# The first stage of an attention + two-MLP kernel: all its instructions in an order written by a list maker

## The chip, the cores and the metric

The kernel runs on one core of a Trainium2 chip. The metric is device time in microseconds (us) of one execution. Five engines run beside each other, each in its own order: PE (matmul), DVE (vector), ACT (activations), POOL (GpSimd) and SP, which issues most of the transfers (DMAs). PE's weight loads are listed as PEld.

## The reference, cut to what matters

```python
a = softmax(phi, axis=2)                       # (4, 8, 576, 32), over the 576 positions
k_m, v_m = a^T k, a^T v                        # (4, 8, 32, 64): pooled keys and values
attn = softmax(q k_m^T / 8, axis=-1) v_m       # (4, 8, 576, 64) -> x: (2304, 512)
h = x @ w_in;  x = (h * cos(h)) @ w_out        # 512 -> 2048 -> 512; w_in and w_out come as float64
p = domain_probs / sum(domain_probs)           # (2304, 4)
out = sum_e p[:, e] * (relu(x @ w1[e]) @ w2[e])  # 4 experts, 512 -> 1024 -> 512
```

## The kernel before, in words

The work has two stages. **Stage one** holds attention and the cosine MLP. Each of the 4 batches has 8 heads in two groups g of 4 (a *part* is one batch and group, eight in all); the positions of a batch fall into two halves th of 288. For each part `pool_exp` takes the exponential of phi (ACT) and transposes it on PE (tiles `pe`, `pt`, copied to `es`), `pool_kv` pools k and v (`kvp`), scales and turns the result (`kvs`, `pkt`) and copies it to `kT` and `vT` (DVE); `scores` multiplies q by kT (`sc`) and runs the softmax in blocks of 32: DVE transpose, max, POOL subtract, ACT Exp, DVE sum, POOL multiply, DVE transpose, and a split into a high and a low fp32r half, `attnT`. `project` folds v_m into a slice of w_in: v_m times w_in, 256 hidden columns at a time (`vw_ps`, split to `vw`). The MLP has 8 such slices, slots s. A *unit* is one slot, batch and half, 64 in all: `hidden1` makes hp = attnT x vw with 12 matmuls (three products of high and low halves each, `mm3`), then h cos h by a chain ACT, ACT, DVE, ACT (Sin), DVE, and a split into `gt` (ACT high, POOL low); `output1` multiplies by w_out (`wo`), 24 matmuls into `op`, and adds to `acc` in SBUF (DVE). The cosine takes the turns h/2pi, rounds them with a large constant and subtracts.

The float64 weights are brought as pairs of 32-bit words and made float32 by `narrow`: one ACT pass and three DVE passes per piece (L116 to L128); `load_out` also splits wo (`split_w`).

**Stage two** combines x into seven operands (`build_x`: `put` writes `x`, ACT high and DVE low half) and multiplies them with seven combinations of w1 (`load2`, `hidden2`, a scheme with seven products in place of eight), then relu and w2 (`output2`), scaled by p_all on DVE. p_all comes by `load_probs`, a transfer asked for by POOL and four small DVE operations.

What sets the order: the whole program is written in the order of the calls at L375 to L433, and a scheduler with a model of the engines then places every instruction of every engine, within the buffers of the pools. The transfers of the first part of stage one stand on SP's queue, the later weight pieces on ACT's.

The chain of one unit, and the calls that the change touches:

```python
marks.append(nc.scalar.activation(out=y, in_=hv, func=ACTF.Copy, scale=INV_2PI, bias=0.25))   # L320
nc.scalar.activation(out=kk, in_=y, func=ACTF.Copy, bias=ROUND)                               # L321
nc.vector.scalar_tensor_tensor(out=y, in0=kk, scalar=ROUND, in1=y, op0=ALU.subtract, op1=ALU.subtract)  # L322
nc.scalar.activation(out=y, in_=y, func=ACTF.Sin, scale=-TWO_PI)                              # L323
nc.vector.tensor_tensor(out=y, in0=hv, in1=y, op=ALU.mult)                                    # L324
```

Of the kernel before, what the change touches and what calls it, by code (L numbers as in the profile page):

```python
# [11 lines left out]
U32 = mybir.dt.uint32  # L12
I64 = mybir.dt.int64
# [6 lines left out]
TWO_PI = 6.283185  # L20
ROUND = 12582912.0
# [3 lines left out]
def tile_kernel(  # L25
# [81 lines left out]
    def narrow(w, src, after=None, part=None):  # L107
        n, m = w.shape[1:]
        c = 1024 // (2 * m)
        for i in range(0, n, c) if part is None else (part * c,):  # L110
            raw = cw.tile([128, c, 2 * m], U32, tag="raw64", name="raw64")
            with tc.issue_after(after.ins) if after else nullcontext():
                (nc.scalar if after else nc.sync).dma_start(out=raw, in_=src[:, i:i + c])
            lo, hi = (raw.rearrange("p a (b t) -> p a b t", t=2)[:, :, :, t] for t in range(2))
            hif = raw.bitcast(F32).rearrange("p a (b t) -> p a b t", t=2)[:, :, :, 1]
# [13 lines left out]

# [41 lines left out]

    kTs, ees = {}, {}

    def pool_exp(b, g):
        ph = phs[b, g]
        nmx = at.tile([128, 1], F32, tag="nmx", name="nmx", bufs=2)
        nc.vector.tensor_reduce(out=nmx, in_=ph, axis=AX.X, op=ALU.max)
        nc.vector.tensor_scalar_mul(nmx, nmx, -1.0)
        ex = ph
        rs = at.tile([128, 1], F32, tag="rs", name="rs", bufs=2)  # L180
        nc.scalar.activation(out=ex, in_=ph, func=ACTF.Exp, bias=nmx, accum_out=rs)
        nc.vector.tensor_scalar_add(rs, rs, 1e-9)
        nc.vector.reciprocal(out=rs, in_=rs)
        es = at.tile([128, NC + 1, 128], F32, tag="es", name="es", bufs=2)
# [195 lines left out]
    for g in range(2):  # L380
        pool_exp(0, g)
# [289 lines left out]
```

## Time and profile before

| | |
|---|---|
| device time, median of 3 runs | 1185.77 us (1185.19 to 1185.85) |
| device time of the profiled execution | 1186.1 us |
| its span, first to last instruction | 1184.3 us |
| PE busy | 1149.7 us (97%) |
| DVE, ACT, POOL busy | 816.6, 474.0, 520.8 us |
| mean granted TensorE clock | 0.98 |

PE's busy share over the whole span hides that the stages differ: the first 125 us and the rest have to be read apart. A busy microsecond of PE at half the clock does half the work, so the granted clock (1.00 is 2.4 GHz, 0.50 is 1.2 GHz) is read beside it. Lines are those of the kernel before.

### The profile page before, as it was taken

Reading aid. Unit: us, or ns where it says so; the run is one execution under the profiler, and the core shown is the slowest. Engines: PE = TensorE matmul, PEld = TensorE weight load, DVE = VectorE, ACT = ScalarE, POOL = GpSimd, SP = SyncE. Lnnn points to the kernel's source line nnn. Section 1 sums busy time; section 2 is a strip of 40 time slices with the busy share of each in tenths; the row PEclk is TensorE's granted clock in tenths of the full one; section 3 lists DMA queues with packets and bytes.
Section 4 is the critical chain, followed back from the end, with each engine's and each line's share of the span. In section 5 each row is a group of like instructions: output and inputs, shape, how many; then the busy total and the mean of one; then the engine's idle time right before and its main releaser. Section 6 shows DMA issues by size and latency. Waiting matters only on the chain.

```text
span 1184.3 us, 19402 instructions
## 1 busy us (share of the span) xinstructions
PE 1149.7 (97%) x7786; PEld 1029.5 (87%) x7786; DVE 816.6 (69%) x1364; ACT 474.0 (40%) x789; POOL 520.8 (44%) x597
## 2 busy tenths in 40 slices
PE   6798999999999989999999999999999999999998
PEld 4467999999999978989898989898989898989897
DVE  4797778877887796666656665696566666666665
ACT  2866556656666632222222222252222223222320
POOL 1455223323328715445444544465445444544420
PEclk8689999999999999999999999999999999999999
DMA  9830111211121101111111111112111111111102
GB/s 316 296 128 2 37 37 37 72 57 35 53 72 55 54 15 40 36 55 54 36 37 54 54 37 36 54 64 106 37 54 54 37 36 54 55 36 36 54 1 80
DMA packets 38842, 72.85 MB, mean 62 GB/s; under 512 B 2624, under 2 KB 20064, under 8 KB 38752
## 3 DMA queue, kind: packets, MB, share of 16 engines
q1 hardware_dynamic: 34208, 58.99, 15.3%
q10 hardware_dynamic: 4480, 12.58, 3.2%
q8 instruction: 61, 1.00, 0.4%
q0 software_dynamic: 64, 0.04, 0.1%
q14 instruction: 29, 0.24, 0.1%
HBM read 66.88 MB, written 4.72 MB: 60 GB/s over the span
## 4 chain that ended last, share of the span: by engine, by line
PE 83%; DVE 5%; DMA 4%; POOL 3%; ACT 3%; issue 2%; SPq 0%; POOLq 0%; ACTq 0%; DVEq 0%
PE op L132 46%; PE hp L132 35%; DMA raw<-in_w_out_dram 2%; PE vw_ps L288 1%; POOL gt L89 1%; DMA q<-in_qt_dram 1%; POOL wa L505 1%; DVE x L462 1%; DMA kvt<-in_kvt_dram 1%; DVE raw L118 1%; DVE y L324 0%; ACT L323 0%; DVE raw L117 0%; DMA raw<-in_w_in_dram 0%; POOL wo L96 0%
## 5 line engine op out<-in xcount | busy, mean ns | idle before, releaser
L132 PE MATMUL op<-wb,ht 128*128 128x512 f32 x1728 | 439.4, 396 | 0.0
L132 PEld LDWEIGHTS hp<-x,wa 128*128 128x128 f32 x2688 | 380.2, 189 | 25.4 <-DVE x L462 4.1
L132 PE MATMUL hp<-x,wa 128*128 128x256 f32 (+1 forms) x2688 | 393.6, 295 | 4.1 <-DVE x L462 3.4
L132 PEld LDWEIGHTS op<-wb,ht 128*128 128x128 f32 x1728 | 312.7, 188 | 58.4
L594 DVE SCALAR_TENSOR_TENSOR acc<-op,p_all,acc 128x512 f32<-128x512 f32 x270 | 201.7, 748 | 136.2 <-PE op L132 136.1
L132 PE MATMUL op<-gt,wo 128*128 128x288 f32 x1536 | 224.1, 299 | 2.2 <-POOL gt L89 1.2
L132 PEld LDWEIGHTS op<-gt,wo 128*128 128x128 f32 x1536 | 210.4, 189 | 12.2 <-issue 3.9
L96 POOL TENSOR_TENSOR wb<-raw,wb 128x256 fp32r<-128x256 f32 x124 | 90.0, 757 | 223.5 <-ACT wb L94 223.5
L565 ACT ACTIVATE ht<-c 128x256 fp32r<-128x256 f32 (+3 forms) x128 | 71.9, 562 | 283.4 <-DVE c L535 283.4
L89 POOL TENSOR_TENSOR gt<-y,gt 128x576 fp32r<-128x576 f32 x64 | 98.2, 1534 | 174.3 <-ACT gt L88 144.1
L566 DVE SCALAR_TENSOR_TENSOR ht<-c,ht 128x256 fp32r<-128x256 f32 (+3 forms) x128 | 94.0, 735 | 63.8 <-ACT ht L565 63.8
L505 POOL TENSOR_TENSOR wa<-raw,wa 128x256 fp32r<-128x256 f32 x96 | 69.3, 749 | 152.2 <-ACT wa L495 152.2
L132 PE MATMUL hp<-attnT,vw 128*128 128x288 f32 x768 | 117.1, 300 | 5.1 <-DVE y L324 5.1
L535 DVE TENSOR_TENSOR c<-hp,u 128x256 f32<-128x256 f32 (+1 forms) x192 | 87.3, 457 | 42.1 <-PE hp L132 37.9
L132 PEld LDWEIGHTS hp<-attnT,vw 128*128 128x128 f32 x768 | 107.2, 190 | 10.2 <-DVE y L324 6.6
L505 POOL TENSOR_TENSOR wa<-tt,wa 128x256 fp32r<-128x256 f32 x128 | 111.0, 896 | 1.2 <-ACT wa L499 1.2
L346 DVE TENSOR_TENSOR acc<-op,acc 128x576 f32<-128x576 f32 x112 | 83.7, 751 | 24.0 <-PE op L132 22.6
L542 ACT COPY p<-hp 128x256 f32<-128x256 f32 x64 | 25.6, 400 | 108.3 <-PE hp L132 108.3
L322 DVE SCALAR_TENSOR_TENSOR y<-kk,y 128x576 f32<-128x576 f32 x64 | 56.9, 890 | 12.9 <-ACT kk L321 12.3
L495 ACT ACTIVATE wa<-raw 128x512 fp32r<-128x512 f32 x32 | 20.2, 632 | 90.0 <-PE hp L132 88.1
L320 ACT ACTIVATE y<-hp 128x576 f32<-128x576 f32 x64 | 41.4, 647 | 36.1 <-PE hp L132 31.7
L323 ACT ACTIVATE y<-y 128x576 f32<-128x576 f32 x64 | 43.7, 682 | 29.2 <-DVE y L322 29.1
(89 smaller groups left out, 915.5 us busy)
## 6 DMA issues: line engine op xcount, KB each, us to landing
raw<-in_w_dram SPq DMA_DIRECT2D x60, 512.0 KB, 3.5
kv<-in_kv_dram SPq DMA_DIRECT2D x16, 512.0 KB, 8.5
raw<-in_w_in_dram ACTq DMA_DIRECT2D x10, 512.0 KB, 3.3
raw<-in_w_out_dram ACTq DMA_DIRECT2D x10, 512.0 KB, 3.2
q<-in_qt_dram SPq DMA_DIRECT2D x8, 576.0 KB, 7.5
out_dram<-acc SPq DMA_DIRECT2D x18, 256.0 KB, 2.0
raw<-in_w_in_dram SPq DMA_DIRECT2D x6, 512.0 KB, 7.2
raw<-in_w_out_dram SPq DMA_DIRECT2D x6, 512.0 KB, 4.9
```

Source lines behind the costliest of these rows:

```text
L89: (eng or nc.vector).tensor_tensor(out=lo, in0=src, in1=f32(hi), op=ALU.subtract)
L96: (nc.vector if early and c % 512 else nc.gpsimd).tensor_tensor(out=t[:, 1, c:c + 256], in0=src[:, c:c + 256], in1=f32(t[:, 0, c:c + 256]) ...
L132: nc.tensor.matmul(out=ps, lhsT=lt(a), rhs=rt(b), start=first and i == 0, stop=last and i == 2, skip_group_check=more,)
L320: marks.append(nc.scalar.activation(out=y, in_=hv, func=ACTF.Copy, scale=INV_2PI, bias=0.25))
L322: nc.vector.scalar_tensor_tensor(out=y, in0=kk, scalar=ROUND, in1=y, op0=ALU.subtract, op1=ALU.subtract)
L323: nc.scalar.activation(out=y, in_=y, func=ACTF.Sin, scale=-TWO_PI)
L346: nc.vector.tensor_tensor(out=dst, in0=op[:, :, :TH], in1=dst, op=ALU.add)
L505: pool.tensor_tensor(out=wa[:, 1, o], in0=src, in1=f32(wa[:, 0, o]), op=ALU.subtract)
L535: nc.vector.tensor_tensor(out=out, in0=ps[:, :n], in1=sb, op=ALU.add)
L565: nc.scalar.activation(out=ht[:, 0, fc, lo:], in_=c[:, fc, lo:], func=ACTF.Relu)
L566: nc.vector.scalar_tensor_tensor(out=ht[:, 1, fc, lo:], in0=c[:, fc, lo:], scalar=0.0, in1=f32(ht[:, 0, fc, lo:]), op0=ALU.max, op1=ALU.su ...
L594: nc.vector.scalar_tensor_tensor(out=dst, in0=op, scalar=pe, in1=dst, op0=ALU.mult, op1=ALU.add)
```

## The change

The scheduler's order of stage one is replaced. Stage one is now written as tasks, Python generators: `queue` (all transfers, on SP), `part` for each of the eight parts, `narrow_in`, `narrow_out`, `project` and `half` for each unit. Each yields its next step as an `Op` (engine, a duration in ns, what it depends on) or a `Ring` (a place in a buffer pool). `Order.run` keeps a clock per engine in the build, always takes the step that can start first, lets one of a lower rank go ahead if it could start within half of the other's duration (not on PE), and emits it; the instructions of each engine stand in that order (`manual_schedule`). `QUEUE` is the order of the first transfers (p phi, k kv, q q, i w_in, o w_out), written out by hand, `RANKS` that of the first tasks. Stage two is left to the scheduler as before.

Beside the order, single steps change. `narrow` loses one of its three DVE passes: the ACT pass is a Prelu that scales positive and negative high words differently, so that one shift-and-or gives the word with its sign. The cosine's turns are rounded by writing `kk` as int32 from hp (ACT), and DVE subtracts it from hp + 0.25; the factor 1/2pi sits in `vw`, 2pi in the last product, so one ACT pass goes. k and v are copied together into `kvT`, the scale of the scores moves into the Exp; the maximum of phi is negated where it is made. For the first slot the op blocks are copied to acc by DVE or ACT, whichever is free. wo's low half is made by POOL in all slots. `load_probs` moves behind the last unit.

```diff
+QUEUE = """p01 i00 p00 k001 i01 k000 q00 k010 o00 k011 q01 q11 p10 k100 k111 o01 q10 i10 k101 p11
+p20 k110 p21 k200 i11 k201 k301 q21 k211 p30 o11 q20 o10 q31 k300 q30 k210 k310 k311 p31""".split()
+RANKS = "u10 A10 A00 A11 A01 u01 wo0 u00 u20 wi1 P1 A20 P0 wi0 A31 P23 u11 A21 A30 u21 wo1".split()
+RINGS = dict(phi=3, kv=4, q=4, raw=2, wi=2, wf=1, wo=2, es=2, st=2, stT=1, kvs=1, vw=2, y=2, kk=1, gt=3, h=2, o=2, c=2, p2=2)
+WAIT = {"PE": 0.0, "ACT": 0.5, "DVE": 0.5, "POOL": 0.5, "SP": 0.5}
...
+            t, _, eng, task = min(heads, key=lambda h: h[:2])
+            edge = t + WAIT[eng] * task[2].ns
+            for t2, rank, eng2, task2 in heads:
+                if eng2 == eng and rank < task[0] and t2 < edge:
+                    t, task = t2, task2
+                    break
...
-            nc.scalar.activation(out=hif, in_=hif, func=ACTF.Copy, scale=2.0 ** -112)
-            nc.vector.tensor_single_scalar(lo, lo, 29, op=ALU.logical_shift_right)
-            nc.vector.scalar_tensor_tensor(
-                out=lo, in0=hi, scalar=3, in1=lo, op0=ALU.logical_shift_left, op1=ALU.bitwise_or
-            )
-            nc.vector.scalar_tensor_tensor(
-                out=w[:, i:i + c].bitcast(U32),
-                in0=hi,
-                scalar=0x80000000,
-                in1=lo,
-                op0=ALU.bitwise_and,
-                op1=ALU.bitwise_or,
-            )
+        o1 = yield Op(
+            "ACT", 690, lambda: nc.scalar.activation(
+                out=hif, in_=hif, func=ACTF.Prelu, scale=2.0 ** -112, alpha=2.0 ** 32), t)
+        o2 = yield dve(430, lambda: nc.vector.tensor_single_scalar(lo, lo, 29, op=ALU.logical_shift_right), t,
+                       port=True)
+        o3 = yield dve(685, lambda: nc.vector.scalar_tensor_tensor(
+            out=w[:, i * c:i * c + c].bitcast(U32), in0=hi, scalar=3, in1=lo,
+            op0=ALU.logical_shift_left, op1=ALU.bitwise_or), o1, o2, *deps, port=True)
...
+        o = yield dve(420, lambda: nc.vector.tensor_copy(
+            out=kvT[b][p0:p0 + 64], in_=pkt[p0:p0 + 64].rearrange("p u (i m) -> p u i m", i=HG)), o)
...
+        o = yield Op("ACT", 650, lambda: marks.append(
+            nc.scalar.activation(out=kk, in_=hv, func=ACTF.Copy, bias=0.25)), o, t0)
...
+        o = yield dve(755, lambda: nc.vector.scalar_tensor_tensor(
+            out=y, in0=hv, scalar=0.25, in1=kk, op0=ALU.add, op1=ALU.subtract), o, t0)
...
+        o = yield act(685, y, y, ACTF.Sin, o, table="sin", scale=SIN_2PI)
+        o = yield dve(755, lambda: nc.vector.scalar_tensor_tensor(
+            out=y, in0=hv, scalar=TWO_PI, in1=y, op0=ALU.mult, op1=ALU.mult), o)
...
+    with tc.manual_schedule():
+        warm_up(25)
+        todo.at["PE"] = 8500.0
+        todo.add(-1, queue())
...
+        todo.run(lambda: all(("part", b, g) in done for b in range(B) for g in range(2)))
...
+        todo.run()
+        load_probs()
```

Where instructions now stand, at three places.

PE, the stretch that ends with the first op blocks (kvp pools k and v, sc are scores, hp and op the two products of a unit, pe and pt the transposes of phi, pkt that of the pooled k and v). Before, from the pooling of batch 2 on:

```order
L202 MATMUL kvp<-kv,es 32x128 x16
L202 MATMUL kvp<-kvt,es 32x128 x4
L218 MATMUL pkt<-ident,kvs 128x128 x2
L202 MATMUL kvp<-kv,es 32x128 x16
L202 MATMUL kvp<-kvt,es 32x128 x4
L240 MATMUL sc<-q,kT 32x288 x8
L218 MATMUL pkt<-ident,kvs 128x128 x2
L187 MATMUL pe<-ident,phi 128x128 x4
L132 MATMUL op<-gt,wo 128x288 x6
```

And now, up to the pooling of batch 2, group 0:

```order
L233 MATMUL hp<-attnT,vw 128x288 x12
L441 MATMUL pkt<-ident,kvs 128x128 x2
L471 MATMUL sc<-q,kvT 32x288 x4
L534 MATMUL vw_ps<-wi,kvT 32x256 x8
L233 MATMUL op<-gt,wo 128x288 x12
L471 MATMUL sc<-q,kvT 32x288 x4
L534 MATMUL vw_ps<-wi,kvT 32x256 x16
L233 MATMUL op<-gt,wo 128x288 x30
L393 MATMUL pe<-ident,phi 128x128 x4
L233 MATMUL op<-gt,wo 128x288 x6
L400 MATMUL pt<-ident,phi 64x128
L419 MATMUL kvp<-kv,es 32x128 x16
```

48 op matmuls, which stood behind both poolings of batch 2, now stand ahead of the first of them.

SP, the end of the first transfers (raw64 are pieces of w_in and w_out; a tile's number only tells it from others of its name). Before, with kv_730 and kv_734 for batch 3, group 0, and kv_867 and kv_871 for its group 1:

```order
L113 DMA raw64_518<-in_w_out_dram 128x1024
L162 DMA kv_730<-in_kv_dram 128x1024
L162 DMA kv_734<-in_kv_dram 128x1024
L164 DMA kvt_732<-in_kvt_dram 64x256
L164 DMA kvt_736<-in_kvt_dram 64x256
L113 DMA raw64_524<-in_w_out_dram 128x1024
L162 DMA kv_867<-in_kv_dram 128x1024
L162 DMA kv_871<-in_kv_dram 128x1024
L164 DMA kvt_869<-in_kvt_dram 64x256
L164 DMA kvt_873<-in_kvt_dram 64x256
L113 DMA raw64_1549<-in_w_in_dram 128x1024
```

And now, with kv_736 for batch 3, group 0, kv_753 for batch 2, group 1, and kv_886 and kv_901 for batch 3, group 1:

```order
L258 DMA q_609<-in_qt_dram 128x1152
L258 DMA kv_736<-in_kv_dram 128x1024
L258 DMA kvt_737<-in_kvt_dram 64x256
L258 DMA q_746<-in_qt_dram 128x1152
L258 DMA kv_753<-in_kv_dram 128x1024
L258 DMA kvt_754<-in_kvt_dram 64x256
L258 DMA kv_886<-in_kv_dram 128x1024
L258 DMA kvt_887<-in_kvt_dram 64x256
L258 DMA kv_901<-in_kv_dram 128x1024
L258 DMA kvt_902<-in_kvt_dram 64x256
L258 DMA phi_920<-in_phi_dram 128x576
L258 DMA raw64_924<-in_w_in_dram 128x1024
```

The transfers are the same ones. What moved is that all weights of the first two slots now stand ahead of these rows, that q and phi come as late as the kv they belong to, and that pieces of batches 2 and 3 alternate.

DVE, the change of stage (acc is the sum of stage one, x the operands of stage two, p_sum and p_all the probabilities). Before:

```order
L346 TENSOR_TENSOR acc<-op,acc 128x2x288 x5
L462 TENSOR_TENSOR x_0_4703<-acc,x_0_4703 128x512
L462 TENSOR_TENSOR x_5_4710<-sB,x_5_4710 128x512
L462 TENSOR_TENSOR x_4_4713<-sA,x_4_4713 128x512
L475 TENSOR_TENSOR sB<-acc,sB 128x512
L462 TENSOR_TENSOR x_3_4721<-acc,x_3_4721 128x512
L454 TENSOR_TENSOR sA<-acc 128x512
L462 TENSOR_TENSOR x_1_4724<-acc,x_1_4724 128x512
```

And now:

```order
L642 TENSOR_TENSOR acc<-op,acc 128x2x288 x4
L204 TENSOR_REDUCE p_sum<-p_all 128x18
L717 TENSOR_TENSOR x_0_4604<-acc,x_0_4604 128x512
L205 TENSOR_SCALAR p_sum<-p_sum 128x18
L717 TENSOR_TENSOR x_5_4611<-sB,x_5_4611 128x512
L206 RECIPROCAL p_sum<-p_sum 128x18
L717 TENSOR_TENSOR x_4_4614<-sA,x_4_4614 128x512
L717 TENSOR_TENSOR x_3_4622<-acc,x_3_4622 128x512
L730 TENSOR_TENSOR sB<-acc,sB 128x512
L207 TENSOR_TENSOR p_all<-p_all,p_sum 128x72
L717 TENSOR_TENSOR x_1_4625<-acc,x_1_4625 128x512
```

The four operations on the probabilities, which stood among the first dozen of DVE's list, now stand between the x tiles; the reduction of p_all is ahead of all of them.

## Rows read from the trace of the kernel before

**Rows 1.** Windows: us busy of PE, PEld, DVE, ACT, POOL; granted clock, DMA share, GB/s.

```profile
0.00:50.00 50.00, 36.55 (x367) 23.91 (x367) 29.46 (x87) 25.44 (x45) 13.42 (x22) 0.78 0.98 323
50.00:75.00 25.00, 19.93 (x172) 12.13 (x166) 23.54 (x48) 14.57 (x25) 17.45 (x16) 0.61 0.67 230
75.00:125.00 50.00, 44.90 (x418) 38.40 (x417) 37.05 (x65) 37.49 (x53) 26.05 (x19) 0.97 0.01 1
125.00:400.00 275.00, 272.71 (x2315) 259.88 (x2315) 220.80 (x308) 171.25 (x256) 114.43 (x94) 1.00 0.16 53
```

**Rows 2.** Windows: the tile hp alone (two rows), then the tile op.

```profile
0.00:60.00 60.00, 4.56 (x24) 3.48 (x24) 1.49 (x2) 1.27 (x2) 0.74 0.92 307
60.00:125.00 65.00, 19.07 (x108) 16.47 (x108) 5.96 (x8) 5.80 (x9) 0.90 0.17 54
...
60.00:125.00 65.00, 26.63 (x165) 24.22 (x166) 10.88 (x21) 0.90 0.17 54
```

**Rows 3.** Timeline of PE: start, us, instructions merged.

```profile
64.79 1.81 PE L132 MATMUL op<-gt,wo 128*128 128x288 f32 x6 [0.57 <-DVE rs L182]
...
76.16 0.60 PE L187 MATMUL pe<-ident,phi 128*128 128x128 f32 x4
76.69 1.17 PE L240 MATMUL sc<-q,kT 64*32 64x288 f32 x16
...
78.03 1.08 PE L202 MATMUL kvp<-kv,es 128*32 128x128 f32 x32
79.04 0.42 PE L202 MATMUL kvp<-kvt,es 64*32 64x128 f32 x8
...
97.08 1.10 PE L288 MATMUL vw_ps<-wi,vT 64*32 64x256 f32 x32
...
114.32 8.15 PE L132 MATMUL op<-gt,wo 128*128 128x288 f32 x60
```

**Rows 4.** Groups by line, whole span: count, busy us and mean ns, idle before.

```profile
L89 POOL TENSOR_TENSOR gt<-y,gt 128x576 fp32r<-128x576 f32 x64 | 98.2, 1534 | 174.3 <-ACT gt L88 144.1 <-issue 27.6 <-PE op L132 2.5
...
L322 DVE SCALAR_TENSOR_TENSOR y<-kk,y 128x576 f32<-128x576 f32 x64 | 56.9, 890 | 12.9 <-ACT kk L321 12.3 <-POOL wa L505 0.3
L324 DVE TENSOR_TENSOR y<-hp,y 128x576 f32<-128x576 f32 x64 | 47.9, 749 | 8.7 <-ACT y L323 7.8
L321 ACT ACTIVATE kk<-y 128x576 f32<-128x576 f32 x64 | 43.7, 683 | 1.5
L323 ACT ACTIVATE y<-y 128x576 f32<-128x576 f32 x64 | 43.7, 682 | 29.2 <-DVE y L322 29.1
...
L320 ACT ACTIVATE y<-hp 128x576 f32<-128x576 f32 x64 | 41.4, 647 | 36.1 <-PE hp L132 31.7 <-POOL gt L89 4.3
```

**Rows 5.** The same view: the DVE pass of the narrowing that goes.

```profile
L118 DVE SCALAR_TENSOR_TENSOR raw<-raw 128x512 uint32<-128x512 uint32 x32 | 23.6, 736 | 0.6 <-ACT raw L116 0.4
```

**Rows 6.** Groups by line from 0 to 130 us: the table loads.

```profile
L323 ACT ACT_TABLE_LOAD x6 | 7.7, 1283 | 0.1
L254 ACT ACT_TABLE_LOAD x4 | 5.1, 1283 | 0.1
L181 ACT ACT_TABLE_LOAD x2 | 2.6, 1283 | 3.7 <-DMA phi<-in_phi_dram 3.7
```

**Rows 7.** Timeline at the change of stage: POOL, DVE, PE.

```profile
410.52 1.44 POOL L89 TENSOR_TENSOR gt<-y,gt 128x576 fp32r<-128x576 f32 x1 [1.14 <-ACT gt L88]
...
416.00 0.76 DVE L346 TENSOR_TENSOR acc<-op,acc 128x576 f32<-128x576 f32 x1 [0.84 <-PE op L132]
...
421.02 3.84 PE L132 MATMUL hp<-x,wa 128*128 128x256 f32 x18 [1.92 <-DVE x L462]
```

**Rows 8.** Timeline of DVE: the longest of the four on the probabilities.

```profile
10.22 0.27 DVE L82 RECIPROCAL p_sum<-p_sum 128x18 f32<-128x18 f32 x1
```

**Rows 9.** DMA issues: count, KB each, us from issue to landing.

```profile
out_dram<-acc SPq DMA_DIRECT2D x18, 256.0 KB, 2.0
...
p_all<-in_probs_dram POOLq DMA_DIRECT2D x1, 36.0 KB, 8.4
```

More of the change, by code (lines that the diff above doesn't have):

```diff
@@ L19, with __init__, free, take @@
 INV_2PI = 1.0 / (2.0 * math.pi)
-TWO_PI = 6.283185
-ROUND = 12582912.0
+TWO_PI = 2.0 * math.pi
+SIN_2PI = 6.283185
+LOG = []
+class Op:
+    def __init__(self, eng, ns, fn, *deps, table=None, port=False):
+        self.engs = eng.split("|")
+        self.ns, self.fn, self.table, self.port = ns, fn, table, port
+        self.ready = max([0.0, *(d.end if isinstance(d, Op) else d for d in deps)])
+class Ring:
+    def __init__(self, n):
+        self.n, self.ends = n, []
+    def free(self):
+        k = len(self.ends) - self.n
+        return k < 0 or self.ends[k] is not None
+    def take(self):
+        k = len(self.ends) - self.n
+        self.ends.append(None)
+        return len(self.ends) - 1, 0.0 if k < 0 else self.ends[k]
+    def give(self, k, end):
+        self.ends[k] = end.end if isinstance(end, Op) else end
+    def idle(self):
+        return all(e is not None for e in self.ends)
@@ L226, in scores, with have, sp, act @@
-    def scores(b, g, split_th):
-        aT, p0 = attnT[b], 64 * g
-        kT = kTs[b]
+    todo = Order()
+    done = {}
+    marks = []
+    def have(*keys):
+        return Until(lambda: all(k in done for k in keys))
+    def sp(out, in_, nbytes, *deps):
+        return Op("SP", nbytes * DMA_NS, lambda: nc.sync.dma_start(out=out, in_=in_), *deps)
+    def act(ns, out, in_, func=ACTF.Copy, *deps, table=None, **kw):
+        return Op("ACT", ns, lambda: nc.scalar.activation(out=out, in_=in_, func=func, **kw), *deps, table=table)
@@ new lines, in dve, with pool, load @@
+    def dve(ns, fn, *deps, port=False):
+        return Op("DVE", ns, fn, *deps, port=port)
+    def pool(ns, fn, *deps):
+        return Op("POOL", ns, fn, *deps, port=True)
+    R = {name: Ring(n) for name, n in RINGS.items()}
+    tiles = {}
+    def load(ring, key, shape, parts, pool_=None, dtype=F32, tag=None, bufs=None):
+        k, t0 = yield R[ring]
+        pool_ = pool_ or at
+        name = tag or ring
+        t = pool_.tile(shape, dtype, tag=name, name=name, **({"bufs": bufs} if bufs else {}))
+        tiles[key] = t, ring, k
+        op = None
+        for out, in_, nbytes in parts(t):
+            op = yield sp(out, in_, nbytes, t0)
+        done[key] = op.end
@@ new lines, in tile_kernel, with narrow_part @@
+    wi, wo = {}, {}
+    def narrow_part(kind, s, i, w, *deps):
+        yield have((kind, s, i))
+        raw, ring, k = tiles[kind, s, i]
+        lo, hi = (raw.rearrange("p a (b t) -> p a b t", t=2)[:, :, :, t] for t in range(2))
+        hif = raw.bitcast(F32).rearrange("p a (b t) -> p a b t", t=2)[:, :, :, 1]
+        t = done[kind, s, i]
+        c = 2 if kind == "in" else 1
+        o1 = yield Op(
[6 more added lines that the diff above has]
+            op0=ALU.logical_shift_left, op1=ALU.bitwise_or), o1, o2, *deps, port=True)
+        R[ring].give(k, o3)
+        return o3
```

633 lines of the change are left out of this document (379 added, 254 removed).

## The prediction

> **What bounds the kernel now.** I read the windows first, to find the poor stretch, then PE's timeline inside it, the groups by line, the DMA issues and the timeline at the change of stage.
>
> The windows [rows 1] say where time can be won. From 125 to 400 us PE is busy 272.71 of 275 us at clock 1.00: nothing is left there but 2.3 us. Before 125 us it is busy 36.55 of 50, 19.93 of 25 and 44.90 of 50 us, so 13.4 + 5.1 + 5.1 = 23.6 us are idle; and the granted clock is 0.78, 0.61 and 0.97, which costs about 36.55 x 0.22 + 19.93 x 0.39 + 44.90 x 0.03 = 17.1 us more. So **some 41 us** are lost before 125 us, and that is the most that a better order of this stretch can give back. The DMA engines are 0.98 busy until 50 us and only 0.67 from 50 to 75 us: at first the data set the pace, then the order does. The count of matmuls [rows 2] shows what was late: 24 of hp and none of op before 60 us, where the first op starts at 64.79 us [rows 3], so the output blocks, which need no more data, were not used to fill PE while the data came.
>
> **A common mark.** At 125 us PE had done all eight attention parts, six projections, 24 + 108 = 132 hp matmuls and 165 of op [rows 2]. I look for the moment at which the changed order has done as much. In its PE list that is the op block of twelve that stands right before the projection of batch 3 for the first two slots (the seventh and eighth): up to it there are 120 hp and 192 op. A matmul of op takes 8.15/60 = 0.136 us [rows 3], and hp is of the same shape, so its list is 27 x 0.136 - 12 x 0.136 = 2.1 us ahead of the old state, and the old kernel stands there at 125 + 2.1 = 127.1 us.
>
> **When does PE become dense?** In the changed PE list the last thing that waits for a transfer of the first kind is the pooling matmul (kvp) of batch 2, group 1; behind it come the pooling of both groups of batch 3 (group 1 some 17 us of PE work later, so that its own transfers have time) and otherwise work whose data are there. Its last piece, the second kv half, is the 14th kv transfer of the queue. With it SP has asked for 7 phi (288 KiB), 8 raw (512), 8 q (576), 14 kv (512) and 14 kvt (64): 18,784 KiB, 19.2 MB, by the shapes of the tiles. The old kernel moved 323 GB/s over its first 50 us, start included [rows 1], so 19.2 MB take **59.5 us** if the queue never waits. It will wait: there are four kv buffers, and the last kv transfers need buffers that the pooling of batch 2, group 0 frees, which stands behind two hp units and 48 op matmuls. The bounds are 0 and the 0.33 x 25 = 8.2 us of DMA time that the old kernel lost between 50 and 75 us [rows 1]. I take 3.5, below the middle, since only two or three transfers are held up: **63 us**.
>
> **From there to the mark.** The list holds 72 hp and 144 op, 216 x 0.136 = 29.4 us; three poolings of 1.08 + 0.42 = 1.5; six blocks of scores at 1.17/2, 3.5; two projections, 1.1; five groups of transposes of at most 0.6, 2.0 [rows 3]. That is 40.5 us at full clock. Stalls on top lie between 0 and what the old kernel lost from 75 to 125 us, 5.1 idle and 1.3 of clock [rows 1], 6.4. I take 2, in the lower half: in the new list op and hp blocks stand between the scores of one part and what needs them. The mark falls at 63 + 40.5 + 2 = 105.5 us instead of 127.1: **-21.6 us**.
>
> **The single edits in this stretch.** They are inside those 40.5 us and count only through the stalls. The cosine loses one ACT pass (L321, 683 ns), and its DVE step (L322, 890 ns, two operands in SBUF) becomes one that reads PSUM and an int32 tile, for which I take L324's 749 ns; ends 749 and 890 [rows 4]. Ten units until the mark save 6.8 us of ACT and about 1.4 of DVE, nothing of PE. Eight narrowings lose L118, 8 x 0.736 = 5.9 us of DVE [rows 5]; the Prelu that replaces Copy is priced at the same ACT pass, since the built list shows no table load beside it. Twelve table loads were run by 130 us [rows 6]; the changed ACT list has eight up to the mark, 4 x 1.283 = 5.1 us less. Against that ACT takes on twelve copies of op that DVE did. k and v leave PSUM in one DVE copy instead of two (kT and vT), a few tenths per part, with the scale moved into the Exp for nothing. The weight loads of later slots go from ACT's queue to SP's, which has nothing else to do then, and from the third slot on POOL alone makes the low half of wo (12 pieces off DVE); it is busy 114.43 of 275 us there [rows 1].
>
> **After the mark.** From hp to the first op of the same unit the new chain is 0.647 (L320) + 0.749 + 0.682 (Sin) + 0.749 + 0.682 (the copy to gt, of Sin's shape and engine) + 1.534 (POOL) = 5.04 us [rows 4], without handovers and queues; the old one had 0.683 + 0.141 more. What PE has between the two, counted in both lists as matmuls times 0.136 us, is 8.25 to 11 us for most units in both, but 6.6 us for six units of the new list where the old one has 7.0 at the least. Such a unit waits if handovers and queues exceed 1.6 us. I take +1 us in all; ends -1 (half of the 2.3 us of idle goes) and +6 (0.1 us per unit over the 54 that are left).
>
> **The change of stage.** Four small operations on p_all and p_sum, once done in the idle start, now stand on DVE around the first x tiles, and there PE waits for DVE: 1.92 us before the 421.02 us matmul [rows 7]. Each is at most 0.27 us [rows 8]; +0.9 us, between 0 and 1.1. And p_all's own transfer is now asked for by POOL behind the last gt. In the old trace that gt ends at 410.52 + 1.44 = 411.96 and the last add of acc at 416.76 us [rows 7]; p_all's reduction stands right behind that add, so the transfer has 4.8 us. Before, it took 8.4 us from issue to landing, while a 256 KB output takes 2.0 [rows 9]. Lateness lies between 0 and 3.6 us. The 8.4 us fell in the 0.98-busy start, the mean DMA share from 125 to 400 us is 0.16 [rows 1]: I take 0. Nothing else of the second stage moves: its own lists are the same.
>
> **Sum.** -21.6 + 1 + 0.9 = -19.7 us on the profiled execution's 1186.1 us (a span of 1184.3 and 1.8 around it) gives 1166.4 us; that execution is 0.3 us over the median of the runs shown. I say **1166 us**.
>
> **A rule that speaks against it.** p_all's 8.4 us were measured in the first 10 us [rows 8, 9]; at its new place DVE is loaded, 220.80 of 275 us [rows 1]. The Trainium skill, "SBUF — State Buffer", section "SBUF: two separate sides", says that a transfer from GpSimd's queue starves while DVE runs operations that take both port pairs, because GpSimd then cannot write the descriptors. No row here shows it either way, as p_all was asked for once, in the start. Without the rule lateness is 0 in the sum; by the rule the transfer would not be faster than at the start. That is the third rival.
>
> **The rivals.**
> *The order is rigid and the data are late.* If the kv buffers hold the queue the full 8.2 us and the stalls reach 6.4, the mark is at 59.5 + 8.2 + 40.5 + 6.4 = 114.6 us, a gain of 12.5; with +1 and +0.9, and 1 to 3 us of stalls more in the slots behind, about 1177. For it: ACT and DVE run in the order written, and an Exp that waits for a late pooling holds the Sin behind it. Against: from 75 to 125 us DVE is busy 37.05 and ACT 37.49 of 50 us [rows 1], which leaves room. Chance 0.20.
> *Everything fits.* No wait of the queue, no stall: mark at 100 us, -27.1 + 0.9, and 1 us less after it: 1159. Chance 0.15.
> *p_all late.* DVE stands still at the change of stage for 3.6 us, and PE behind it: 1170. Chance 0.08.
> *Slower: the short lags bite all through the first stage.* The new order starts op blocks closer behind their hp. If queues on DVE and ACT stretch the 5.04 us chain beyond what PE has in between, PE stops once per unit. The point at which it eats the gain is 19.7/54 = 0.37 us per unit; at 0.7 us the time is 1166 + 0.7 x 54 = 1204. For it: DVE is busy 220.80 of 275 us there. Against: the old list ran the same DVE load with nearly the same lags and left 2.3 us idle [rows 1]. Chance 0.05.
> *No change.* The order makes no difference because the data arrive when they arrive and the catching up after 75 us was already dense: 1186. Against: 44.90 of 50 us busy, but on work that could have been done before. Chance 0.04.
> What is left for the forecast itself: 0.48.
>
> **How the numbers follow.** The forecast's own range is 1161 to 1172 (3.5 +- 3 us of queue wait, 2 +- 2 of stalls, +-2 behind). The range that should hold 8 in 10 takes in "everything fits", p_all late and most of the rigid case: **1156 to 1179**; below 1156 would need data faster than 323 GB/s as well. About 0.2% (2.4 us) is what a measurement can tell from no change. Faster by more: the forecast, 0.48, "fits", 0.15, p_all, 0.08, and nearly all of the rigid case, 0.19: 0.90. Within: 0.04 and a tail of the rigid case, 0.05. Slower: 0.05.
>
> **What would show it.** In the changed profile: op's first matmul between 42 and 50 us (64.79 before); the first-stage transfers at an end by 66 to 70 us; the mark (165 op matmuls done) near 101 to 105 us instead of 125; PE's idle and clock loss before 125 us down from 41 to about 19 us; eight table loads until the mark; from 125 to 400 us idle of PE at most 3.5 us; at the change of stage DVE not waiting for p_all. The forecast is wrong in its main step if PE is not dense from about 63 us on, and wrong in its second if the windows from 125 us on lose more than 4 us. The slower case would show as a stop before an op block, released by POOL, once per unit.

## The result, and the profile after

The changed kernel takes 1166.88 us (median of 4, 1164.58 to 1169.47) against 1185.72 us (1185.19 to 1185.85): a ratio of 0.9843, 95% interval 0.9818 to 0.9867. The profile is of the 1164.58 us execution, the fastest of the four, whose span is 1162.8 us; before it was 1184.3. Run again later beside the kernel before, it gave 0.9826 (0.9813 to 0.9840).

The windows of the changed kernel, columns as in [rows 1]:

```profile
0.00:50.00 50.00, 40.04 (x420) 28.52 (x420) 30.77 (x74) 26.31 (x46) 17.82 (x26) 0.80 0.92 312
50.00:75.00 25.00, 21.66 (x257) 16.30 (x259) 20.75 (x42) 19.68 (x37) 15.62 (x14) 1.00 0.70 247
75.00:125.00 50.00, 47.77 (x435) 42.41 (x434) 35.17 (x64) 32.77 (x51) 21.47 (x16) 1.00 0.06 20
125.00:400.00 275.00, 268.62 (x2282) 258.67 (x2281) 197.90 (x280) 143.94 (x218) 118.53 (x107) 1.00 0.16 52
```

Before 125 us PE is idle for 9.96 + 3.34 + 2.23 = 15.5 us, and the clock costs 40.04 x 0.20 = 8.0 more: 23.5 us where 41 were lost (I had named about 19). From 50 to 75 us the clock is 1.00 instead of 0.61. The last window now holds the change of stage, so its 6.4 us of idle are not to be set against the old 2.3; up to 300 us it has none.

The same view for the tile op [rows 2]:

```profile
0.00:60.00 60.00, 7.41 (x48) 6.49 (x48) 0.92 (x2) 2.29 (x6) 0.83 0.91 310
60.00:125.00 65.00, 32.87 (x220) 29.97 (x221) 9.03 (x19) 4.97 (x10) 1.00 0.19 63
```

By 60 us 48 op matmuls are done, where there were none. PE's timeline, columns as in [rows 3]:

```profile
44.29 1.86 PE L233 MATMUL op<-gt,wo 128*128 128x288 f32 x12
...
53.60 1.08 PE L419 MATMUL kvp<-kv,es 128*32 128x128 f32 x32
...
56.33 0.44 PE L441 MATMUL pkt<-ident,kvs 128*128 128x128 f32 x2 [1.29 <-ACT kvs L261]
...
64.06 1.08 PE L419 MATMUL kvp<-kv,es 128*32 128x128 f32 x32 [0.18 <-DVE rs L406]
...
102.56 3.54 PE L233 MATMUL op<-gt,wo 128*128 128x288 f32 x24 [0.72 <-DVE acc L642]
...
106.66 1.86 PE L233 MATMUL op<-gt,wo 128*128 128x288 f32 x12 [0.55 <-DVE acc L642]
...
110.03 1.85 PE L233 MATMUL hp<-attnT,vw 128*128 128x288 f32 x12 [0.49 <-DVE y L597]
```

op starts at 44.29 us instead of 64.79. The kvp of batch 2, group 1 starts at 64.06 us, and what held it last was DVE, not a transfer. The op block of twelve at 106.66 us closes my mark (120 hp, 192 op); what follows it starts at 108.44 us, so the mark is at 108.4 us, against 127.1 in the old kernel. The hp block at 110.03 us stands right behind it, after a projection, in every list below that keeps this order, and I use its start as a ruler.

Groups by line up to 110 us, for [rows 4, 6]:

```profile
L603 POOL TENSOR_TENSOR gt<-y,gt 128x576 fp32r<-128x576 f32 x9 | 13.2, 1462 | 11.4 <-ACT gt L261 11.4
...
L261 ACT ACT_TABLE_LOAD x8 | 10.3, 1283 | 3.8 <-DMA phi<-in_phi_dram 3.6
...
L593 DVE SCALAR_TENSOR_TENSOR y<-hp,kk 128x576 f32<-128x576 f32 x10 | 7.4, 739 | 1.1 <-ACT kk L590 1.0
...
L590 ACT ACTIVATE kk<-hp 128x576 int32<-128x576 f32 x10 | 6.5, 649 | 6.2 <-PE hp L233 4.2 <-DVE y L593 2.0
```

Eight table loads, as forecast, so the Prelu brings none of its own; the new DVE step takes 739 ns, for which I had 749. The change of stage, for [rows 7]:

```profile
389.62 1.43 POOL L603 TENSOR_TENSOR gt<-y,gt 128x576 fp32r<-128x576 f32 x1 [3.36 <-ACT gt L261]
390.99 1.38 POOL L202 DMA_DIRECT2D p_all<-in_probs_dram  x1
...
394.46 0.76 DVE L642 TENSOR_TENSOR acc<-op,acc 128x576 f32<-128x576 f32 x1 [0.84 <-PE op L233]
395.35 0.23 DVE L204 TENSOR_REDUCE p_sum<-p_all 128x18 f32<-128x72 f32 x1
...
399.58 0.86 PE L233 MATMUL hp<-x,wa 128*128 128x256 f32 x5 [1.64 <-DVE x L717]
```

and p_all's transfer among the DMA issues, 4.3 us from issue to landing where [rows 9] had 8.4:

```profile
p_all<-in_probs_dram POOLq DMA_DIRECT2D x1, 36.0 KB, 4.3
```

It lands as DVE ends its last add, at 395.3 us. From the last gt to the end of the span it is 1162.8 - 389.6 = 773.2 us, before 1184.3 - 410.5 = 773.8: the second stage gave and took next to nothing. But for these 0.6 us all of the gain is there by 390 us.

### The profile page after: what moved, and what is told of

Same layout as the page of the kernel before. It is cut to its first block, busy times and chain, and to the rows that moved or that the text cites. A ratio compares the mean times of both kernels' runs of the same rounds, so it can differ in the third digit from the quotient of the medians.

```text
span 1162.8 us, 19304 instructions
## 1 busy us (share of the span) xinstructions
PE 1134.9 (98%) x7786; PEld 1022.7 (88%) x7786; DVE 772.9 (66%) x1291; ACT 435.6 (37%) x741; POOL 516.9 (44%) x609
## 4 chain that ended last, share of the span: by engine, by line
PE 91%; DVE 4%; DMA 2%; POOL 2%; ACT 1%; issue 0%; SPq 0%; ACTq 0%; POOLq 0%
PE op L233 50%; PE hp L233 38%; DMA kv<-in_kv_dram 1%; PE vw_ps L534 1%; PE kvp L419 1%; DVE x L717 1%; PE sc L471 1%; POOL gt L603 1%; POOL wa L760 0%; DMA p_all<-in_probs_dram 0%; POOL attnT L507 0%; DVE y L597 0%; DMA raw<-in_w_dram 0%; DVE smx L485 0%; DVE st L482 0%
## 5 line engine op out<-in xcount | busy, mean ns | idle before, releaser
L603 POOL TENSOR_TENSOR gt<-y,gt 128x576 fp32r<-128x576 f32 x64 | 94.2, 1473 | 157.8 <-ACT gt L261 123.0
L642 DVE TENSOR_TENSOR acc<-op,acc 128x576 f32<-128x576 f32 (+1 forms) x119 | 85.7, 721 | 59.0 <-PE op L233 57.2
L593 DVE SCALAR_TENSOR_TENSOR y<-hp,kk 128x576 f32<-128x576 f32 x64 | 48.0, 750 | 18.9 <-ACT kk L590 15.9
L261 ACT ACTIVATE gt<-y 128x576 fp32r<-128x576 f32 x64 | 43.8, 684 | 37.2 <-DVE y L597 37.2
L590 ACT ACTIVATE kk<-hp 128x576 int32<-128x576 f32 x64 | 41.2, 643 | 35.5 <-PE hp L233 33.5
```

Source lines behind the costliest of these rows:

```text
L261: return Op("ACT", ns, lambda: nc.scalar.activation(out=out, in_=in_, func=func, **kw), *deps, table=table)
L590: nc.scalar.activation(out=kk, in_=hv, func=ACTF.Copy, bias=0.25)), o, t0)
L593: o = yield dve(755, lambda: nc.vector.scalar_tensor_tensor(out=y, in0=hv, scalar=0.25, in1=kk, op0=ALU.add, op1=ALU.subtract), o, t0)
L603: o = yield pool(1430, lambda: nc.gpsimd.tensor_tensor(out=gt[:, 1], in0=y, in1=f32(gt[:, 0]), op=ALU.subtract), o)
L642: e = yield dve(150 + 303 * nd, lambda: nc.vector.tensor_tensor(out=dst, in0=op[:, :, :TH], in1=dst, op=ALU.add), o)
```

## The experiments

My theory going in was that the listed order makes the gain, above all by op blocks that fill PE while the data come; the first rival was that the saved passes of ACT and DVE make it. Ratios are to the kernel before on the same chip.

**1. The operations alone**, in the old kernel, whose scheduler then places all instructions anew:

```diff
-        marks.append(nc.scalar.activation(out=y, in_=hv, func=ACTF.Copy, scale=INV_2PI, bias=0.25))
-        nc.scalar.activation(out=kk, in_=y, func=ACTF.Copy, bias=ROUND)
+        marks.append(nc.scalar.activation(out=kk, in_=hv, func=ACTF.Copy, bias=0.25))
...
-            nc.scalar.activation(out=hif, in_=hif, func=ACTF.Copy, scale=2.0 ** -112)
+            nc.scalar.activation(out=hif, in_=hif, func=ACTF.Prelu, scale=2.0 ** -112, alpha=2.0 ** 32)
...
```

> The kernel before, in its own order, with the changed operations alone: the cosine by int32 turns (one ACT pass less per unit), the narrowing by two DVE passes instead of three, the scale of 1/(2 pi) moved into vw. k and v still leave PSUM apart. If the order makes the gain (my theory): the stretch before 125 us keeps its losses, op's first matmul stays behind 60 us, and the time is 1181 to 1188 us. If the saved passes make it (rival: 64 x 0.683 us of ACT and the narrowings' third pass, 0.736 us each on DVE): 1164 to 1174 us.

1184.31 us, ratio 0.9998 (0.9989 to 1.0008): in the sum the passes alone bring nothing. The windows of this kernel, though, are not those of the old one:

```profile
0.00:50.00 50.00, 33.89 (x363) 23.33 (x363) 29.48 (x87) 27.06 (x46) 16.29 (x25) 0.84 0.99 334
75.00:125.00 50.00, 48.79 (x452) 40.18 (x452) 37.58 (x67) 29.48 (x40) 22.92 (x17) 1.00 0.03 12
125.00:200.00 75.00, 75.00 (x618) 70.08 (x617) 53.70 (x75) 36.16 (x53) 23.89 (x18) 1.00 0.10 36
200.00:300.00 100.00, 100.00 (x842) 93.42 (x841) 73.55 (x105) 50.57 (x74) 31.30 (x24) 1.00 0.15 54
300.00:400.00 100.00, 100.00 (x823) 94.75 (x823) 75.81 (x103) 52.38 (x77) 52.23 (x53) 1.00 0.17 59
```

From 75 to 400 us PE is idle for 1.2 us instead of 5.1 + 2.3. Against that stand 16.1 us of idle instead of 13.4 in the first 50 us, and projections cut into pieces: from 125 to 400 us PE was busy with vw_ps for 21.31 us (392 matmuls), in the old kernel for 15.45 (416). So this null is a gain and losses in one. Which of them belong to the shorter passes and which to the new placing is not shown, nor what the passes would be worth in the old order as it stood.

**2. The code without its order**:

```diff
-    with tc.manual_schedule():
+    with nullcontext():
```

> The changed kernel, its steps emitted by the same list maker, but the scheduler may move each instruction as it did in the kernel before. If the gain hangs on the listed order: the scheduler puts p_all and some matmuls in other places, op starts later than 44 us, the 125 to 400 us stretch may lose more than 2.3 us, and most of the 18.8 us go: 1176 to 1192 us. If only the sequence of emission and the changed operations matter (rival): 1164 to 1170 us.

1192.26 us, 1.0068 (1.0051 to 1.0086): slower than the kernel before, and just above my range. The windows of this kernel:

```profile
75.00:125.00 50.00, 42.76 (x372) 36.83 (x371) 38.57 (x67) 34.77 (x52) 23.55 (x19) 0.93 0.15 54
125.00:200.00 75.00, 71.77 (x584) 66.62 (x583) 47.91 (x65) 38.44 (x59) 26.09 (x22) 1.00 0.14 50
```

PE loses 7.2 us of 50 and then 3.2 of 75, and from the last gt (412.00 us) to the end it takes 1188.7 - 412.0 = 776.7 us, 3.5 more than in the changed kernel. As material for the scheduler the generators' sequence is a poor one; the gain hangs on the list being obeyed.

**3. op held back**:

```diff
-                o = yield Op("PE", 800 * nd, mm2, og, t0, done["wo", s])
+                o = yield Op("PE", 800 * nd, mm2, og, t0, done["wo", s], 64000.0)
```

> The changed kernel, in whose list no op block may stand before the list maker's own 64 us; all else by the same rules. This undoes the one thing that I said was late before: op blocks as filling while the data come. My theory: op's first matmul at 60 to 68 us instead of 44.3, the clock in 45 to 70 us falls as before (1.00 now, 0.50 to 0.57 before), the mark of 120 hp and 192 op comes 5 to 15 us later than 108.4, the time is 1172 to 1183 us. Rival (the data set the pace anyway, and the op blocks only change places with later work): mark within 2 us, 1164 to 1170 us.

1179.64 us, 0.9957 (0.9942 to 0.9972). PE's timeline, then its windows:

```profile
58.08 3.23 PE L233 MATMUL op<-gt,wo 128*128 128x288 f32 x12
...
123.98 1.09 PE L534 MATMUL vw_ps<-wi,kvT 64*32 64x256 f32 x32
```

```profile
50.00:75.00 25.00, 22.31 (x233) 17.57 (x234) 14.46 (x34) 13.22 (x26) 11.34 (x12) 0.80 0.63 220
75.00:125.00 50.00, 44.73 (x381) 35.89 (x380) 32.00 (x61) 30.15 (x46) 21.24 (x17) 0.90 0.06 22
```

op starts 14 us later, the clock falls again, and the 120 hp and 192 op of the mark are done where the projection at 123.98 us begins: 15.5 us late, just past my 5 to 15. That the data set the pace anyway is out. With these rules and ranks a list without early op blocks loses some 13 us (0.0114 of 1185). But holding them back also makes the whole list anew, with ranks that were written for another one, and experiment 7 shows that a list made anew can cost much; no run tells the two apart.

**4. All saved passes put back** as work, with the first-stage order kept:

```diff
-                out=hif, in_=hif, func=ACTF.Prelu, scale=2.0 ** -112, alpha=2.0 ** 32), t)
+                out=hif, in_=hif, func=ACTF.Copy, scale=2.0 ** -112), t)
...
+        def join():
+            nc.vector.scalar_tensor_tensor(
+                out=lo, in0=hi, scalar=3, in1=lo, op0=ALU.logical_shift_left, op1=ALU.bitwise_or)
+            nc.vector.scalar_tensor_tensor(
+                out=w[:, i * c:i * c + c].bitcast(U32), in0=hi, scalar=0x80000000, in1=lo,
+                op0=ALU.bitwise_and, op1=ALU.bitwise_or)
+
+        o3 = yield dve(685, join, o1, o2, *deps, port=True)
...
+        def turns():
+            nc.scalar.activation(out=kk, in_=hv, func=ACTF.Copy, bias=0.25)
+            marks.append(nc.scalar.activation(out=kk, in_=hv, func=ACTF.Copy, bias=0.25))
+
+        o = yield Op("ACT", 650, turns, o, t0)
```

> The changed kernel in its own first-stage order, with the saved work put back as load: the ACT pass that makes kk runs twice in each of 64 units (+0.65 us each, 41.6 us of ACT), and the narrowing has its three DVE passes again (+0.74 us each). The result is the same. My theory (they lie beside other work; only stalls count): +0 to +4 us over the changed kernel, 1164 to 1171 us. Rival (the saved passes carry the gain): most of the 18.8 us go, 1176 us or more; with the chain from hp to op 0.65 us longer, PE would stop before op blocks in the 125 to 400 us stretch, where it is now idle under 3 us.

1184.08 us, 0.9986 (0.9975 to 0.9998). I had expected +4 us at most; it is +17, and the gain is gone. My theory as I had put it falls: in this order the passes do not all lie beside other work. Of some 65 us put back (64 x 0.65 on ACT, 32 x 0.74 on DVE) about a quarter comes out in the time. The next two kernels split them.

**5 and 6. The narrowing's third pass alone; the ACT pass alone** (the two halves of the diff above).

> The changed kernel in its own first-stage order, with the third DVE pass of each narrowing put back alone (+0.74 us each; eight of them before 110 us, four per slot pair behind). With both sets of passes back the gain was gone (1184.1 us), so one theory fell; this and the next kernel tell which pass carried it. Theory A (DVE is the engine that the listed chains run on; a scaled word that comes later also holds a weight load and its raw buffer): 1173 to 1181 us, with the losses before 200 us. Theory B (the chain from hp to op decides, and the narrowing is not in it): 1166 to 1171 us.

> The changed kernel in its own first-stage order, with only the ACT pass that makes kk run twice in each of 64 units (+0.65 us each; the result is the same). Theory B (the chain from hp to op, 5.0 us by itself, grows by 0.65 us, and the units with the shortest lag stop PE): stops before op blocks released by POOL in all of 125 to 390 us, 5 to 15 us in all, 1172 to 1182 us. Theory A: 1166 to 1172 us.

1174.58 us, 0.9919 (0.9899 to 0.9940), and 1174.07 us, 0.9904 (0.9888 to 0.9921): set against 0.9843 that is 9.0 and 7.2 us (0.0076 and 0.0061 of 1185), with both 16.9, so they add up as far as such differences tell, each of them known to some 4 us. The ruler block (110.03 us) starts at 115.08, 115.81 and, with both, 116.55 us; the last gt (389.62 us) at 399.71, 400.37 and 406.32. So behind the ruler each costs 5 us more and both cost 10: (399.71 - 115.08) - (389.62 - 110.03) = 5.0, then 5.0 and 10.2. Ahead of it they cost 5.0 and 5.8 us, and both only 6.5. What PE waited for from the ruler to the last gt (engine and line, what released it: us in all, times, longest), first in the changed kernel:

```profile
PE op L233 <- POOL gt L603: 3.4, 4, 1.3
PE hp L233 <- DVE y L597: 0.5, 1, 0.5
```

with the narrowing's pass back:

```profile
PE op L233 <- POOL gt L608: 3.4, 5, 1.1
PE hp L233 <- DVE vw L556: 1.3, 1, 1.3
PE hp L233 <- DVE y L602: 1.2, 2, 0.7
PE vw_ps L539 <- DVE y L602: 0.8, 1, 0.8
PE op L233 <- DVE acc L647: 0.7, 1, 0.7
```

and with the ACT pass back:

```profile
PE op L233 <- POOL gt L606: 6.0, 6, 1.9
PE hp L233 <- DVE y L600: 0.5, 1, 0.5
```

Theories A and B each hold for their own pass. A longer narrowing holds DVE, and hp and projections wait for DVE; a longer chain from hp to op stops PE before op blocks, released by POOL, 6.0 us instead of 3.4. That is 3.5 and 2.6 us of the 5. Of the rest, the clock of 0.97 from 340 to 390 us makes some 1.4 us with the ACT pass; what is left, some 1.5 and 1 us, has no wait of its own in these rows. Ahead of the ruler not all of the 5.0 and 5.8 us need be the passes': with the ACT pass the clock stood at 0.50 from 60 to 66 us, which is worth some 3 us, and a shorter fall there is found in an execution of the changed kernel too (12).

**7. Passes back, list told of them**: experiment 4 with `Op("ACT", 1300, ...)` and `dve(1420, ...)`.

> As the kernel with both sets of passes put back, but the list maker is given their durations (1300 instead of 650 ns for the ACT pass, 1420 instead of 685 ns for the last DVE pass), so it writes another order. If the loss came from a list that no longer fitted its operations (theory C, the order is rigid): 1167 to 1174 us. If it came from the work itself (theory D, engines or chains too long for any order of these rules): 1179 to 1188 us.

1202.27 us, 1.0141 (1.0115 to 1.0167): outside both ranges, and 18 us worse than the list that was not told. The longest stop, in PE's timeline:

```profile
114.15 3.22 PE L233 MATMUL hp<-attnT,vw 128*128 128x288 f32 x12 [5.62 <-DVE y L605]
```

Theories C and D both miss. Besides the durations a table of ranks makes the list, and that I left as it was: with it, the right durations do not give a good list. Whether other ranks could hold the gain with the old passes is open; no run tries it.

**8. A fifth kv buffer**, laid into the half of acc that is written later:

```diff
+        j = k % 5 - 4
+        if j < 0:
...
+            a = acc[:, NT * KD // 2 + 1280 * j:][:, :1280].rearrange("p (c u d) -> p c u d", u=2, d=2 * D)
+            t, t2 = a[:, :NC], a[:TAIL, NC]
```

> The changed kernel with a fifth kv buffer, laid into the half of acc that is first written later; the listed order of PE, ACT, DVE and POOL hardly moves. SP waited 17.3 us for kvp to free kv buffers, and I had put the delay of the dense part at 3.5 us for it. If that wait holds PE: the kvp of batch 2, group 1 and all behind it come 2 to 5 us earlier, 1162 to 1165 us. If the waiting transfers were hidden (PE's stops at 56 to 69 us are all put down to ACT and DVE, none to a DMA): within 1 us, 1165 to 1168 us.

1166.6 us, 0.9844 (0.9829 to 0.9858): no difference. The DMA share up to 50 us rises from 0.92 to 0.99, and still SP waits for kvp, later in the queue:

```profile
SPq L258 <- PE kvp L424: 19.5, 5, 10.0
```

The second half of the kv of batch 2, group 1, the fourteenth kv transfer, is asked for 2.6 us earlier; SP's timeline of the changed kernel, then of this one:

```profile
57.44 0.42 SPq L258 DMA_DIRECT2D kv<-in_kv_dram  x1
```

```profile
54.84 0.33 SPq L258 DMA_DIRECT2D kv<-in_kv_dram  x1
```

So the transfers ran ahead, the wait as such only moved, and PE's stops stayed the same ones, released by ACT and DVE: what SP waits for there is hidden. (In this profile the kvp that started at 64.06 us starts at 67.17, as the clock stood at 0.50 from 58 to 65 us; up to the pkt before that fall, at 56.44 us against 56.33, PE is where it was.)

**9. PE kept busy in its waits**:

```diff
+    def fill(ps, n):
+        for _ in range(n):
+            nc.tensor.matmul(out=ps, lhsT=ones, rhs=ones, start=True, stop=True)
...
         def pooled():
+            fill(kvp, {(0, 0): 1, (0, 1): 8}.get((b, g), 0))
```

> The changed kernel with 21 matmuls on ones put into eight places where PE waits (each 0.33 us as in the warm-up; eight before the second kvp, where PE waits 2.93 us for a kv transfer, and one to four elsewhere, each into the PSUM tile that the next matmul starts afresh). The clock fell to 0.50 at 17 us after that wait and came back at 37 us; in the profile of the kernel with the fifth buffer it fell once more, from 58 to 65 us, behind the 1.3 us wait at 55 us. Theory G (the clock is lost to these waits, and the first-stage work is on the path): clock 1.00 from 17 to 37 us and at 58 us, first op 2 to 5 us earlier than 44.3, 1160 to 1164 us, and the runs of one kernel lie closer together than 5 us. Rival H (between 17 and 37 us PE only waits longer for its data when it is faster): the first op within 1.5 us of 44.3, 1164 to 1168 us.

1164.23 us, 0.9831 (0.9814 to 0.9847). Its timeline:

```profile
19.94 1.07 PE L424 MATMUL kvp<-kv,es 128*32 128x128 f32 x28 [1.58 <-DMA kv<-in_kv_dram]
...
43.60 1.85 PE L233 MATMUL op<-gt,wo 128*128 128x288 f32 x12
```

The clock stayed at 1.00 until about 21 us and was back at 32 instead of 37, and yet op starts only 0.7 us earlier, and no earlier than in the unaltered kernel of experiment 12 (43.47 us). Rival H: between 17 and 37 us a faster PE waits longer for the others.

**10. No table loads** (another function is computed):

```diff
-        o = yield act(685, y, y, ACTF.Sin, o, table="sin", scale=SIN_2PI)
+        o = yield act(685, y, y, ACTF.Exp, o, table="sin", scale=SIN_2PI)
```

> The changed kernel with Exp in place of Sin in the cosine (so it computes another function), which takes seven of the eight table loads up to 105 us away, 7 x 1.283 = 9.0 us of ACT, and moves no instruction on any engine. With 6.5 us of ACT passes put back up to the mark, 5 to 6 us were lost by 125 us, so ACT looked to be on the path there. Theory E (it is): 3 to 8 us earlier at the mark, 1158 to 1164 us. Rival F (the listed order is only hurt by longer operations and not helped by shorter ones, as PE then waits for DVE or for data): within 1.5 us, 1165 to 1168 us.

1163.45 us, 0.9814 (0.9799 to 0.9828). The ruler block:

```profile
107.23 1.85 PE L233 MATMUL hp<-attnT,vw 128*128 128x288 f32 x12 [0.49 <-DVE y L597]
```

It starts 2.8 us earlier for 9.0 us less of ACT, and no instruction moved: a little under theory E's lower edge. By the last gt 1.7 us of it are left (387.88 against 389.62 us), and while the time lies in E's range, its interval overlaps that of the unaltered kernel in experiment 12. ACT looks to be on the path there, but at most a third of what is taken from it comes out.

**11 and 12. PE kept busy and load_probs at the start of the list; the changed kernel again**:

```diff
+        load_probs()
         warm_up(25)
...
         todo.run()
-        load_probs()
```

> The kernel with PE kept busy in eight waits, and with load_probs moved from behind the first stage to its start, so that p_all's transfer and its four small DVE operations leave the change of stage. My term for them there was +0.9 us (0 to 1.1), with p_all itself not late: so 0.5 to 1.5 us less from the last gt to the end of the span (773.2 us in the changed kernel), 1162.5 to 1164 us. Rival (p_all's 4.3 us transfer was what DVE and PE waited for behind the last gt): 2 to 4 us less, 1160 to 1162 us. Rival (the four operations were hidden behind the additions to acc, and in the start they delay the first nmx): 1164 to 1166 us.

> The changed kernel, unaltered, on the same chip as the kernel above. It tells what that kernel's difference is worth, and why executions of the changed kernel lie 5 us apart (1164.6 to 1169.5) where those of the kernel before lay within 0.7. Theory G: the clock falls a second time, near 58 us, in some executions: 1165 to 1168 us, spread over 3 us or more, while the kernel with PE kept busy spreads less. Rival: the spread is the chip's, and both kernels spread alike.

1169.17 us, 0.9863 (0.9849 to 0.9878), and 1164.98 us, 0.9826 (0.9813 to 0.9840). Early probabilities cost some 4 us: 0.0032 of 1185 against experiment 9, 0.0037 against the changed kernel on the same chip. DVE's timeline of experiment 11:

```profile
10.20 0.23 DVE L204 TENSOR_REDUCE p_sum<-p_all 128x18 f32<-128x72 f32 x1 [9.19 <-DMA p_all<-in_probs_dram]
...
11.12 0.74 DVE L384 TENSOR_REDUCE nmx<-phi 128x1 f32<-128x576 f32 x1
```

its transfer:

```profile
p_all<-in_probs_dram POOLq DMA_DIRECT2D x1, 36.0 KB, 8.9
```

and PE's first transposes, which start at 9.12 us in the changed kernel:

```profile
14.21 1.94 PE L397 MATMUL pe<-ident,phi 128*128 128x128 f32 x8 [5.39 <-ACT phi L261]
```

The first nmx stood at 3.57 us; behind an operation that waits 9.19 us for a slow transfer it stands at 11.12. The last gt comes at 393.34 us instead of 388.82. The last rival is right, and dearer than I had put it. From there to the end it is 1166.5 - 393.3 = 773.2 us, in experiment 9 1162.3 - 388.8 = 773.5, in the changed kernel 773.2 and, run again, 773.0: at the change of stage the four operations cost nothing that these profiles show.

In the profile of experiment 12, the unaltered kernel, the clock fell a second time, to 0.50 from about 69 to 72 us, which the first profile does not show. Its window:

```profile
50.00:75.00 25.00, 21.93 (x248) 16.31 (x247) 19.39 (x41) 18.19 (x33) 14.84 (x14) 0.93 0.71 243
```

and that of experiment 8:

```profile
50.00:75.00 25.00, 21.69 (x232) 15.34 (x231) 17.82 (x38) 17.99 (x33) 12.52 (x12) 0.86 0.55 179
```

Five runs each spread over 2.4 us here and 2.8 with PE kept busy, and the kernel before, on the same chip, over 2.8 (1184.27 to 1187.10): all three spread alike, as the rival had it, and that the fall makes a part of the spread is not shown. Experiment 9's interval (0.9814 to 0.9847) and this one's overlap almost wholly: filling the waits gives nothing that can be told apart, and no version here beats the changed kernel beyond doubt.

## Why the prediction was right, and where it was not

The time was right: 1166 forecast, 1166.88 measured. On the profiled execution I had -19.7 us, and its span is 21.5 us shorter; it is the fastest of four, and the medians are 18.8 us apart. The steps, on the profiled execution:

- **Common mark and dense part.** First op 42 to 50 us: 44.29. Kvp of batch 2, group 1 at 63 us: 64.06. Mark at 105.5: 108.4, so -18.7 us instead of -21.6. Of the 2.9 us that are missing 1.1 lie ahead of that kvp, and 108.4 - 64.06 - 40.5 = 3.8 us stand where I took 2 of stalls, inside the ends of 0 and 6.4; 2.7 of them are idle time (PE is busy for 41.64 of 44.38 us there), the rest is work that took longer than my 40.5. In experiment 3 a list without early op blocks loses some 13 us, though not by their absence alone as far as is shown.
- **The 3.5 us for the kv buffers.** The number fitted, the reason did not. The data did come about when I said: the last of them is asked for at 57.44 us, and the DMA share falls from 0.86 (60 to 62 us) to 0.06 (62 to 64 us), so they were there by about 62 us. But PE did not wait for them. From 56.33 to 64.06 us it stands idle for only 0.8 us, kvp was held by DVE at the end, no stop of PE behind 18.54 us is put down to a transfer, and transfers that were asked for earlier (experiment 8) moved nothing. That kvp starts at 64 us because PE's own list gets there then; that this and the transfers come out alike is luck.
- **The single edits, costed at nothing.** This is the step that failed. I named the cover, "inside those 40.5 us" of PE work, and added that they count only through the stalls, without asking whether the 2 us of stalls that I took were possible without them. Experiments 4 to 6 show that with the passes back about 17 us go: in a list in which nothing may move aside, some of the 0.65 to 0.74 us that each pass takes on ACT or DVE comes out on PE. Experiments 1 and 2 show the other half, that the passes or the code alone gain nothing where the scheduler places the instructions. The gain belongs to both together, and these runs book no part of it to one alone.
- **After the mark.** +1 forecast (-1 to +6). From the mark to the last gt the old kernel took 410.5 - 127.1 = 283.4 us, the new one 389.6 - 108.4 = 281.2: -2.2 us. The stops are where I said, before op blocks and released by POOL, four of them, 3.4 us, against 2.3 us of idle before. What more than made up for that is PE's busy time, 277.7 us with 2386 matmuls and before 280.5 us with 2376; 1.2 us of it lie in the 416 matmuls of the projections (14.23 us against 15.45), most of the rest in op (187.64 us for 1316 against 189.88 for 1319). Why the same matmuls took less is open, but the 2.3 us of idle were not all that was left there, as I had read the window.
- **Change of stage.** +0.9 forecast: -0.6 measured, with the four operations at nothing that the profiles show (experiment 11 against 9). p_all took 4.3 us where 4.2 were to be had (394.46 + 0.76 - 390.99), so it was 0.1 us late at most, and the rival is out here. The Trainium skill, "SBUF — State Buffer", section "SBUF: two separate sides", says that such a transfer starves while DVE runs operations that take both port pairs; no run here tests it, as DVE ran only three adds to acc (0.76 us each, from 390.60, 392.87 and 394.46 us) while this one was under way. The 8.9 us of experiment 11 were not of that kind: DVE ran nothing then.
- **The rivals.** Late data: experiment 8 speaks against it. Everything fits: the mark came at 108.4 us and not at 100. No change and short lags all through the stage are refuted by the time; but experiments 4 and 6 show that the short lags were nearer than the 0.05 that I gave them suggests: with 0.65 us more in the chain the stops released by POOL behind the ruler grow from 3.4 us to 6.0 and 5.7, though there are six of them, not one per unit.

That the sum came out is in part luck: the mark fell 2.9 us short, and the two terms behind it were 3.2 and 1.5 us better than forecast.

## What to carry to other kernels

Where an order is written down instruction by instruction, a pass is not free because it seems to lie beside other work: whether the order holds depends on the durations in it, so price the edits and the order together, and put one back without the other to see (experiments 4 to 6). A list that was made with a table of ranks can get worse when its maker is given other durations (experiment 7). And where a scheduler places the instructions, an edit of the operations also changes the order, so a null result can be a gain and a loss (experiment 1). In a fixed order never put an operation that waits for a slow transfer ahead of the first work of its engine (experiment 11).

## What the runs showed of the hardware

- The granted clock of one and the same list falls at other times in another execution: first at 16 us in one profile of the changed kernel and at 14 us in the other, and a second time, near 69 us, in the other one alone. In two kernels of the same order it fell a second time at 58 us (experiment 8) and at 60 us (experiment 6), though PE's longest wait shortly before 60 us, 1.3 to 1.4 us before pkt, is nearly the same in all four. Where it stayed at 0.50 for 6 to 7 us, that cost some 3 us.
- p_all's 36 KB took 8.4 and 8.9 us when asked for in the first 2 us, in experiment 11 with DVE idle and a DMA share of about 1.0 from 2 to 10 us, and 4.3 us at 391 us, where the DMA share is at most 0.23.
